# Half-width attention matmuls in alternation on the halves of TensorE's array, and k scores always in 32 bits

## The chip, the cores and the metric

One core of a Trainium2 chip runs the whole kernel. The metric is the device time of one execution in microseconds. Three runs of the kernel before took 1616.36, 1618.4 and 1621.14 us; the median, 1618.4, is the time before.

## What is computed

Three parts in a row, in float32 throughout:

```python
def sm_attn(qq, kk, vv):                       # softmax attention, 8 batches, 8 heads, head size 64
    s = scale * np.matmul(qq, kk.transpose(0, 1, 3, 2))
    s = s - np.max(s, axis=-1, keepdims=True)
    a = np.exp(s)
    a = a / (np.sum(a, axis=-1, keepdims=True) + 1e-09)
    return np.matmul(a, vv)
p_packed = sm_attn(p, k, v)                    # 32 packed queries against 576 keys
out = sm_attn(q, p_packed, p_packed)           # 576 queries against the 32 packed values
...
xk = mu_k * x + (1.0 - mu_k) * x_prev          # first MoE block, x_prev is x moved by one position
xr = mu_r * x + (1.0 - mu_r) * x_prev
k = np.maximum(xk @ w_k, 0.0)
x = 1.0 / (1.0 + np.exp(-(xr @ w_r))) * (k * k @ w_v)
...
h = x.transpose(0, 2, 1) @ U @ V               # second block, rank 32 over the positions
u = x + h.transpose(0, 2, 1)
u + np.maximum(u @ w_ch1, 0.0) @ w_ch2         # 512 to 2048 and back
```

## The kernel before, in words

**Units of attention.** The work of attention is cut into 16 units. Unit u holds two batches (a pair, `bp = u // 4`) and two heads (`j = u % 4`); in code the batch of the pair is `b2`. The two heads of 32 packed queries of one batch fill 64 partitions, and the two batches 128. `attention_steps` (line 641) writes one unit as a row of steps: turn k and p with TensorE transposes into `kh` and `pT`; scores of p against k into two banks of 288 columns (line 684); the exponentials into `a1`, which TensorE turns into `at`; `at` times v (line 739), scaled and masked to `pp`, which is copied to `ppz` (line 747) and turned to `ppt`; scores of q against `ppt` (line 762) and their softmax in `a2`, turned into `th`; and `ppz` times `th` into the output `xo` (line 803).

**Where the two batches of a pair stand on the array.** TensorE has 128 rows (the contraction) and 128 columns (the partitions of the result). For the scores of k, `pT` has four blocks of 64 columns, of which the two outer ones hold a batch each and the two inner ones zeros, so that each batch's 128-column weights fill its own 64 result partitions and add nothing to the others; the matmuls of both batches add up in one bank. `ppz` is laid out alike: `ppz[:, lh, b2, :]` has all 128 rows, those of the other batch being zero. Only `at` times v is written with 64-column weights into its half of the result partitions, first all four of batch 0 and then all four of batch 1.

**Plain and split units.** A matmul on 32-bit operands (F32) leaves two records for one instruction in the profile. The first seven units (`NPLAIN = 7`, "plain") use it everywhere. From unit 7 on ("split") the helper `halves` (line 653) writes an operand as two F32R tiles, its rounded value (on ACT) and the rest (on DVE): `kh` and `kl`, the two planes of `pT`, `th` and `tl`, the two planes of `ppz`. A product is then three one-record matmuls: high with high, high with low, low with high. The profile names all operands f32.

**Order of the work.** Everything is recorded in a `Plan` first, and `emit` (line 333) fixes each engine's program with a model of costs: an operation becomes ready when its inputs are, and of the ready ones the lowest class goes first, then the earliest recorded. Attention has class 0, the MoE blocks class 1, so a unit's matmuls are put among MoE matmuls, ahead of them when both are ready. `copy` (line 275) may go to ACT or DVE, whichever the plan has free. The first four units run interleaved at the start, with all eight PSUM banks (`att_banks`, line 542); after that attention has two banks, `ps_a`, given out in the order of the steps, and units 4 to 15 run under the chunks of the first MoE block, four for each pair of batches. The weights are cast and split on the way (`Cast`, line 821). Big tiles (`kin`, `qin`, `vin`, `kh`, `kl`, `qt`, `at`, `th`, `tl`, `xo`) rotate through one pool of eight buffers; all DMAs are issued on SP, and the loads for the next unit are recorded after the steps that free their tiles.

**Names in the profile.** Matmuls are recorded in one helper (line 197) and transposes in another (line 208), so groups are told apart by tiles: `psat` is attention's bank, `psk`, `psv`, `psr`, `psu` those of the first MoE block, `psc`, `psh`, `pst` those of the second.

Of the kernel before, what the change touches and what calls it, by code (L numbers as in the profile page):

```python
# [9 lines left out]
F32 = mybir.dt.float32  # L10
F32R = mybir.dt.float32r
# [458 lines left out]
def packed_attention_moe_mixer_kernel(  # L470
# [20 lines left out]
    P = 128  # L491
# [16 lines left out]
    plan = Plan(nc)  # L508
    add, sub, mul = ALU.add, ALU.subtract, ALU.mult
# [34 lines left out]
    def ps_att():  # L544
        return plan.bank(att_banks[0], "psat", att_banks[0] is ps_a)
# [17 lines left out]
    class Bufs:  # L563
# [13 lines left out]
            self.kept = None  # L577

        def keep(self, plain):

            if self.kept is None or self.kept[0] != plain:
                dt, n = (F32, 1 if self.first else 2) if plain else (F32R, 2)
                pT = plan.tile(self.one, [P, n, 4, 64], dt, "pT")
                ppz = plan.tile(self.one, [P, n, 2, P], dt, "ppz")
                for b2 in range(2):
                    r = slice(b2 * 64, (b2 + 1) * 64)
                    z = self.a1[r, 576 - b2 * 64:640 - b2 * 64].unsqueeze(1)
                    m = (1 if plain else 2) * 4
                    for t, v in ((pT, "p a b c -> p (a b) c"), (ppz, "p a b (e c) -> p (a b e) c")):
                        w = t[r, 0:m // 4].rearrange(v, **({} if t is pT else {"c": 64}))  # L590
                        plan.copy(w, z.to_broadcast([64, m, 64]), ("dve",))
                self.kept = (plain, pT, ppz)
            return self.kept[1:]

# [46 lines left out]
    def attention_steps(A, u, u_next):  # L641
# [3 lines left out]
            load_p(bp + 1)  # L645
        plan.tt(A.pbd, p_t[bp][:, j, :].unsqueeze(1).to_broadcast([P, 2, D]), hmask, mul)
        plain = u < NPLAIN
        kh = A.big(F32 if plain else F32R, "kh")
        kl = None if plain else A.big(F32R, "kl")
        qt, at = A.big(F32, "qt"), A.big(F32, "at")  # L650
        pT, ppz = A.keep(plain)

        def halves(hi, lo, src):
            if plain:
                plan.copy(hi, src)
            else:
                plan.act(hi, src, AF.Copy)
                plan.tt(lo, src, hi, sub)
# [3 lines left out]
        for b2 in range(2):  # L662
            yield
            ps = ps_att()
            for t in range(4):
                plan.transpose(ps[:, t * P:(t + 1) * P],
                               kin.at(b2)[:, b2 * 512 + t * P:b2 * 512 + (t + 1) * P], ident)
            sl = slice(b2 * 576, b2 * 576 + 512)
            halves(kh[:, sl], None if plain else kl[:, sl], ps)
        yield  # L670
        ps = ps_att()
        plan.transpose(ps[:, 0:P], kin[:, 1024:1152], ident)
        plan.transpose(ps[:, P:2 * P], A.pbd.rearrange("p h d -> p (h d)"), ident)
        pk_ = ps[:, 0:P].rearrange("p (b c) -> p b c", b=2)
        pp_ = ps[:, P:2 * P].rearrange("p (b c) -> p b c", b=2)
        khr = kh.rearrange("p (b c) -> p b c", b=2)[:, :, 512:576]
        halves(khr, None if plain else kl.rearrange("p (b c) -> p b c", b=2)[:, :, 512:576], pk_)
        halves(pT[:, 0, 0::3, :], None if plain else pT[:, 1, 0::3, :], pp_)
        if u_next is not None:
            A.load_k(u_next, A.after)  # L680

# [2 lines left out]
        for c in range(2):  # L684
            yield
            ps = ps_att()
            terms = []
            for b2 in range(2):
                ph = pT[:, 0, 2 * b2:2 * b2 + 2, :].rearrange("p a c -> p (a c)")
                pl = None if plain else pT[:, 1, 2 * b2:2 * b2 + 2, :].rearrange("p a c -> p (a c)")  # L690
                sl = slice(b2 * 576 + c * 288, b2 * 576 + (c + 1) * 288)
                terms += [(ph, kh[:, sl])] if plain else [(ph, kh[:, sl]), (ph, kl[:, sl]), (pl, kh[:, sl])]
            for n, (lh, rh) in enumerate(terms):
                plan.mm(ps[:, 0:288], lh, rh, start=(n == 0), stop=(n + 1 == len(terms)))
            plan.reduce(st[:, c:c + 1], ps[:, 0:288], ALU.max)
            sps.append(ps)
        plan.tt(st[:, 2:3], st[:, 0:1], st[:, 1:2], ALU.max)
# [5 lines left out]
        for b2 in range(2):  # L703
            r = slice(b2 * 64, (b2 + 1) * 64)
# [6 lines left out]
        for c in range(3):  # L711
            yield
            ps = ps_att()
            for t in range(3):
                i = 3 * c + t
                plan.transpose(ps[:, t * P:(t + 1) * P], qin[:, i * P:(i + 1) * P], ident)
            n = 3 if c < 2 else 2
# [9 lines left out]
        ps = ps_att()  # L727
# [4 lines left out]
        ps = ps_att()  # L732
# [3 lines left out]
        yield  # L736
        ps = ps_att()
        vm = vin[:, 0:1024].rearrange("p (b h t d) -> p b h t d", b=2, h=2, t=4)
        for b2 in range(2):
            for t in range(4):  # L740
                plan.mm(ps[b2 * 64:(b2 + 1) * 64, 0:P],
                        at[:, t * P + b2 * 64:t * P + (b2 + 1) * 64], vm[:, b2, :, t, :],
                        start=(t == 0), stop=False, skip_group_check=True)
        plan.mm(ps[:, 0:P], at[:, 512:640], vin[:, 1024:1152], start=False, stop=True, skip_group_check=True)
        pp = plan.tile(A.one, [P, P], F32, "pp")
        plan.stt(pp, ps[:, 0:P], st[:, 9:10], hmask.rearrange("p h d -> p (h d)"), mul, mul)
        for b2 in range(2):
            r = slice(b2 * 64, (b2 + 1) * 64)
            plan.copy(ppz[r, 0, b2, :], pp[r])
            if not plain:  # L750
                plan.tt(ppz[r, 1, b2, :], pp[r], ppz[r, 0, b2, :], sub)
        if u_next is not None:
            A.load_v(u_next, A.after)
        yield
        ps = ps_att()
# [33 lines left out]
        th = A.big(F32 if plain else F32R, "th")  # L789
        tl = None if plain else A.big(F32R, "tl")  # L790
        yield
        ps = ps_att()
# [4 lines left out]
        ps = ps_att()  # L797
        plan.transpose(ps[:, 0:P], a2g[:, 512:640], ident)
        for b2 in range(2):
            r = slice(b2 * 64, (b2 + 1) * 64)  # L800
            halves(th[r, 512:576], None if plain else tl[r, 512:576], ps[r, r])
        xo = A.big(F32, "xo", (0, 1)).rearrange("p (i b c) -> p i b c", i=NI, b=2)
        for b2 in range(2):
            for c0, c1 in ((256, 576), (0, 256)):
                yield
                ps = ps_att()
                w = c1 - c0
                terms = ((0, th),) if plain else ((0, th), (0, tl), (1, th))
                for n, (lh, rh) in enumerate(terms):
                    plan.mm(ps[:, 0:w], ppz[:, lh, b2, :], rh[:, c0:c1], start=(n == 0),  # L810
                            stop=(n + 1 == len(terms)))
                plan.copy(xo.on(b2)[:, c0 // 64:c1 // 64, b2, :],
                          ps[:, 0:w].rearrange("p (i c) -> p i c", c=64))
        plan.dma(x_d[bp].at(j)[j * P:(j + 1) * P, :], xo.rearrange("p i b c -> p (i b c)"))

    def attention(A, u, u_next):
        for _ in attention_steps(A, u, u_next):
            pass
# [93 lines left out]
    plan.cls = 0  # L912
    A0.after = go
    steps = [attention_steps(AX_[u], u, NJ if u == 0 else None) for u in range(NJ)]
    step = 0
    while any(s is not None for s in steps):
# [38 lines left out]
    for b2 in range(2):  # L955
        r = slice(b2 * 64, (b2 + 1) * 64)
        z = A0.a1[r, 576 - b2 * 64:608 - b2 * 64]
# [263 lines left out]
    for n in range(len(chunks)):  # L1221
        b, c = chunks[n]
# [48 lines left out]
    for n in range(len(chunks)):  # L1271
        prep = []
        if n + 1 < len(chunks):
            b1, c1 = chunks[n + 1]
# [4 lines left out]
        for m in range(MC + 2):  # L1279
# [6 lines left out]
            if m >= 6 and prep:  # L1286
                kind, a = prep.pop(0)
# [42 lines left out]
```

## Time and profile before

| what | value |
|---|---|
| median of three runs | 1618.4 us (1616.36 to 1621.14) |
| the profiled execution | 1620.91 us |
| its span, first to last instruction | 1619.1 us |
| busy: PE, DVE, ACT, POOL | 1559.5, 800.2, 616.8, 3.0 us |
| granted TensorE clock, mean over the span | 0.985 of 2.4 GHz |
| DMA | 128.57 MB, 79 GB/s over the span |

PE is TensorE's matmuls, PEld its weight loads. A PE record lasts from its start to its modelled end, latency included, and the next starts before it ends; the time that a matmul takes from the engine is the distance between two starts. A row of the windows table has the stretch, its length in us, and then, for each engine that has work there, in the order PE, PEld, DVE, ACT, POOL, the busy us and in brackets the number of records in flight; the last three numbers are the granted clock (PEclk, 1.00 is 2.4 GHz), the busy share of the 16 DMA engines and GB/s. A row of the timeline has the start in us, the time from the first start to the last end of the records merged in it, the engine, and what they are; "128*64" is the part of the array that is used, rows by columns, and "128x288" the operand that moves through it, partitions by elements. `psat<-kh,pT` reads: written `psat`, read `kh` and `pT`.

### The profile page before, as it was taken

The numbers are of one execution on the slowest core, as the hardware profiler recorded it, in microseconds if no ns is written. First come the engines' busy times: TensorE is split into PE (matmuls) and PEld (weight loads), VectorE is DVE, ScalarE is ACT, GpSimd is POOL, SyncE is SP. The second block draws the span as 40 slices with busy tenths as digits, with TensorE's granted clock in tenths as the row PEclk, the third lists the DMA queues.
The fourth block names the chain that finished last, engine by engine and source line by source line (L and its number), as shares of the span: only waits on it lengthen the run. The fifth ranks groups of instructions, "written<-read, shape, count | busy, mean of one in ns | idle before, by whom it ended". The sixth has DMA issues, their size and how long they took to land.

```text
span 1619.1 us, 21662 instructions
## 1 busy us (share of the span) xinstructions
PE 1559.5 (96%) x8152; PEld 1384.9 (86%) x8152; DVE 800.2 (49%) x2035; ACT 616.8 (38%) x1442; POOL 3.0 (0%) x18
## 2 busy tenths in 40 slices
PE   7777889999999999999999999999999999999998
PEld 6566778888888888888889999999999989999997
DVE  5879887887888778764532222222222222221211
ACT  4767666666766666554321111111111111111110
POOL 0000000000000000000000000000000000000000
PEclk9889899999999999999999999999999999999999
DMA  9965445456453333330511101010010101101000
GB/s 184 214 165 140 124 123 137 136 137 168 132 134 122 128 93 112 109 108 20 167 61 46 46 1 39 1 46 13 27 39 1 40 1 40 40 0 40 0 20 20
DMA packets 156393, 128.57 MB, mean 79 GB/s; under 512 B 94145, under 2 KB 121473, under 8 KB 156289
## 3 DMA queue, kind: packets, MB, share of 16 engines
q1 hardware_dynamic: 156288, 127.19, 27.9%
q8 instruction: 64, 1.05, 0.3%
q14 instruction: 41, 0.33, 0.1%
HBM read 89.33 MB, written 37.82 MB: 79 GB/s over the span
## 4 chain that ended last, share of the span: by engine, by line
PE 91%; DVE 3%; ACT 2%; DMA 2%; SPq 1%; issue 1%; ACTq 0%; DVEq 0%
PE psc L197 49%; PE psv L197 12%; PE psk L197 12%; PE psr L197 6%; PE psat L197 6%; PE psat L208 2%; SPq L311 1%; PE psu L197 1%; PE psh L197 1%; PE pst L208 1%; ACT a L229 1%; DMA qin<-in_q_dram 1%; DMA s<-w_d 0%; DVE h L265 0%; DVE m L250 0%
## 5 line engine op out<-in xcount | busy, mean ns | idle before, releaser
L197 PE MATMUL psc<-ut,w 128*128 128x384 f32 x2304 | 433.9, 338 | 1.0 <-DVE hid L265 1.0
L197 PE MATMUL psc<-w,hid 128*128 128x512 f32 x1728 | 426.1, 393 | 1.1 <-ACT hid L229 1.1
L197 PEld LDWEIGHTS psc<-ut,w 128*128 128x128 f32 x2304 | 405.5, 188 | 13.1 <-DVE hid L265 1.4
L197 PEld LDWEIGHTS psc<-w,hid 128*128 128x128 f32 x1728 | 322.0, 188 | 60.9 <-ACT hid L229 1.5
L265 DVE SCALAR_TENSOR_TENSOR hid<-psc,hid 128x384 fp32r<-128x384 f32 x192 | 106.9, 557 | 466.1 <-ACT hid L229 466.0
L229 ACT ACTIVATE hid<-psc 128x384 fp32r<-128x384 f32 x192 | 94.2, 491 | 607.5 <-PE psc L197 607.5
L197 PE MATMUL psv<-wv,kk 128*128 128x512 f32 x864 | 227.9, 400 | 3.7 <-DVE wv L250 3.7
L197 PE MATMUL psk<-xk,wk 128*128 128x384 f32 x1152 | 227.7, 341 | 1.0 <-DVE xk L250 1.0
L197 PEld LDWEIGHTS psk<-xk,wk 128*128 128x128 f32 x1152 | 202.1, 189 | 7.6 <-DVE xk L250 1.5
L197 PEld LDWEIGHTS psv<-wv,kk 128*128 128x128 f32 x864 | 159.4, 189 | 32.9 <-DVE wv L250 4.3
L197 PE MATMUL psr<-wr,xr 128*128 128x512 f32 x432 | 111.0, 403 | 4.6 <-ACT xr L280 4.6
L197 PEld LDWEIGHTS psr<-wr,xr 128*128 128x128 f32 x432 | 81.6, 193 | 21.3 <-ACT xr L280 4.9
L250 DVE TENSOR_TENSOR kk<-sq,kk 128x384 fp32r<-128x384 f32 x96 | 52.6, 553 | 46.1 <-ACT kk L280 45.5
L229 ACT ACTIVATE sq<-psk 128x384 f32<-128x384 f32 x96 | 46.4, 486 | 69.4 <-PE psk L197 67.7
L229 ACT ACTIVATE m<-x,om_t 128x384 f32<-128x384 f32 x96 | 57.2, 610 | 12.3 <-DVE xk L250 6.0
L262 DVE SCALAR_TENSOR_TENSOR m<-x,mu_t,m 128x384 f32<-128x384 f32 x96 | 57.9, 611 | 3.8 <-ACT m L229 3.6
L250 DVE TENSOR_TENSOR ut<-pst,ut 128x512 fp32r<-128x512 f32 x36 | 24.9, 691 | 67.4 <-ACT ut L229 67.3
L229 ACT ACTIVATE a<-st 128x256 f32<-128x256 f32 (+2 forms) x109 | 45.8, 427 | 23.2 <-DVE m L250 16.5
L250 DVE TENSOR_TENSOR u<-psh,u 128x512 f32<-128x512 f32 x36 | 24.9, 691 | 51.0 <-PE psh L197 47.8
L229 ACT ACTIVATE m<-st 128x256 f32<-128x256 uint32 (+2 forms) x109 | 45.2, 426 | 7.1 <-DVE wv L250 2.7
L250 DVE TENSOR_TENSOR o<-psc,u 128x512 f32<-128x512 f32 x36 | 24.6, 688 | 46.5 <-PE psc L197 44.7
L229 ACT ACTIVATE ut<-pst 128x512 fp32r<-128x512 f32 x36 | 21.5, 598 | 67.6 <-PE pst L208 67.6
(134 smaller groups left out, 1527.3 us busy)
## 6 DMA issues: line engine op xcount, KB each, us to landing
st<-in_moe_w_ch_dram SPq DMA_DIRECT2D x64, 256.0 KB, 2.8
qin<-in_q_dram SPq DMA_DIRECT2D x32, 288.0 KB, 5.3
x_d<-xo SPq DMA_DIRECT2D x16, 576.0 KB, 3.4
x_d<-x SPq DMA_DIRECT2D x36, 256.0 KB, 3.7
u<-x_d SPq DMA_DIRECT2D x36, 256.0 KB, 3.4
out_dram<-o SPq DMA_DIRECT2D x36, 256.0 KB, 2.0
kin<-in_k_dram SPq DMA_DIRECT2D x32, 256.0 KB, 4.5
vin<-in_v_dram SPq DMA_DIRECT2D x32, 256.0 KB, 4.7
```

Source lines behind the costliest of these rows:

```text
L197: self.nc.tensor.matmul(o, l, r, start=start, stop=stop, **k)
L208: self.nc.tensor.transpose(out.get(), in_.get(), ident.get())
L229: self.nc.scalar.activation(o, in_.get(), func, **k)
L250: return self.elem(engs, lambda e, o, x, y: e.tensor_tensor(out=o, in0=x, in1=y, op=op), out, [a, b], self.TT, cls)
L262: ("dve",), lambda e, o, x, y, z: e.scalar_tensor_tensor(out=o, in0=x, scalar=z, in1=y, op0=op0, op1=op1), out, [a, b, s], {"dve": (1.042, ...
L265: ("dve",), lambda e, o, x, y: e.scalar_tensor_tensor(out=o, in0=x, scalar=s, in1=y, op0=op0, op1=op1), out, [a, b], self.TT, cls)
L311: self.nc.sync.dma_start(out=o, in_=i)
```

## The change

- `pT` holds one 32-bit block of 64 columns for each batch, with no zero blocks, and the scores of k become two matmuls for each 288 columns, one into each half of the result partitions (64 columns of the array). This holds for split units too, so `kl` and the low plane of `pT` are gone.
- `at` times v runs over the four pieces outside and the batches inside, so the halves alternate.
- `ppz` holds `pp` once, with no zeros, and is copied once instead of once per batch. The last product takes the 64 rows of each batch from `ppz` and `th`, one batch into each of two banks, alternating; both banks are asked for before the first matmul, and both are copied out after the last.
- The zero fills of `pT` and `ppz` are gone.

```diff
--- before.py
+++ after.py
@@ -577,18 +577,10 @@
             self.kept = None
 
         def keep(self, plain):
-
             if self.kept is None or self.kept[0] != plain:
                 dt, n = (F32, 1 if self.first else 2) if plain else (F32R, 2)
-                pT = plan.tile(self.one, [P, n, 4, 64], dt, "pT")
-                ppz = plan.tile(self.one, [P, n, 2, P], dt, "ppz")
-                for b2 in range(2):
-                    r = slice(b2 * 64, (b2 + 1) * 64)
-                    z = self.a1[r, 576 - b2 * 64:640 - b2 * 64].unsqueeze(1)
-                    m = (1 if plain else 2) * 4
-                    for t, v in ((pT, "p a b c -> p (a b) c"), (ppz, "p a b (e c) -> p (a b e) c")):
-                        w = t[r, 0:m // 4].rearrange(v, **({} if t is pT else {"c": 64}))
-                        plan.copy(w, z.to_broadcast([64, m, 64]), ("dve",))
+                pT = plan.tile(self.one, [P, 2, 64], F32, "pT")
+                ppz = plan.tile(self.one, [P, n, P], dt, "ppz")
                 self.kept = (plain, pT, ppz)
             return self.kept[1:]
 
@@ -645,8 +637,7 @@
             load_p(bp + 1)
         plan.tt(A.pbd, p_t[bp][:, j, :].unsqueeze(1).to_broadcast([P, 2, D]), hmask, mul)
         plain = u < NPLAIN
-        kh = A.big(F32 if plain else F32R, "kh")
-        kl = None if plain else A.big(F32R, "kl")
+        kh = A.big(F32, "kh")
         qt, at = A.big(F32, "qt"), A.big(F32, "at")
         pT, ppz = A.keep(plain)
 
@@ -666,7 +657,7 @@
                 plan.transpose(ps[:, t * P:(t + 1) * P],
                                kin.at(b2)[:, b2 * 512 + t * P:b2 * 512 + (t + 1) * P], ident)
             sl = slice(b2 * 576, b2 * 576 + 512)
-            halves(kh[:, sl], None if plain else kl[:, sl], ps)
+            plan.copy(kh[:, sl], ps)
         yield
         ps = ps_att()
         plan.transpose(ps[:, 0:P], kin[:, 1024:1152], ident)
@@ -674,8 +665,8 @@
         pk_ = ps[:, 0:P].rearrange("p (b c) -> p b c", b=2)
         pp_ = ps[:, P:2 * P].rearrange("p (b c) -> p b c", b=2)
         khr = kh.rearrange("p (b c) -> p b c", b=2)[:, :, 512:576]
-        halves(khr, None if plain else kl.rearrange("p (b c) -> p b c", b=2)[:, :, 512:576], pk_)
-        halves(pT[:, 0, 0::3, :], None if plain else pT[:, 1, 0::3, :], pp_)
+        plan.copy(khr, pk_)
+        plan.copy(pT, pp_)
         if u_next is not None:
             A.load_k(u_next, A.after)
 
@@ -684,14 +675,10 @@
         for c in range(2):
             yield
             ps = ps_att()
-            terms = []
             for b2 in range(2):
-                ph = pT[:, 0, 2 * b2:2 * b2 + 2, :].rearrange("p a c -> p (a c)")
-                pl = None if plain else pT[:, 1, 2 * b2:2 * b2 + 2, :].rearrange("p a c -> p (a c)")
-                sl = slice(b2 * 576 + c * 288, b2 * 576 + (c + 1) * 288)
-                terms += [(ph, kh[:, sl])] if plain else [(ph, kh[:, sl]), (ph, kl[:, sl]), (pl, kh[:, sl])]
-            for n, (lh, rh) in enumerate(terms):
-                plan.mm(ps[:, 0:288], lh, rh, start=(n == 0), stop=(n + 1 == len(terms)))
+                plan.mm(ps[b2 * 64:(b2 + 1) * 64, 0:288], pT[:, b2, :],
+                        kh[:, b2 * 576 + c * 288:b2 * 576 + (c + 1) * 288],
+                        start=True, stop=True, skip_group_check=True)
             plan.reduce(st[:, c:c + 1], ps[:, 0:288], ALU.max)
             sps.append(ps)
         plan.tt(st[:, 2:3], st[:, 0:1], st[:, 1:2], ALU.max)
@@ -736,19 +723,17 @@
         yield
         ps = ps_att()
         vm = vin[:, 0:1024].rearrange("p (b h t d) -> p b h t d", b=2, h=2, t=4)
-        for b2 in range(2):
-            for t in range(4):
+        for t in range(4):
+            for b2 in range(2):
                 plan.mm(ps[b2 * 64:(b2 + 1) * 64, 0:P],
                         at[:, t * P + b2 * 64:t * P + (b2 + 1) * 64], vm[:, b2, :, t, :],
                         start=(t == 0), stop=False, skip_group_check=True)
         plan.mm(ps[:, 0:P], at[:, 512:640], vin[:, 1024:1152], start=False, stop=True, skip_group_check=True)
         pp = plan.tile(A.one, [P, P], F32, "pp")
         plan.stt(pp, ps[:, 0:P], st[:, 9:10], hmask.rearrange("p h d -> p (h d)"), mul, mul)
-        for b2 in range(2):
-            r = slice(b2 * 64, (b2 + 1) * 64)
-            plan.copy(ppz[r, 0, b2, :], pp[r])
-            if not plain:
-                plan.tt(ppz[r, 1, b2, :], pp[r], ppz[r, 0, b2, :], sub)
+        plan.copy(ppz[:, 0, :], pp)
+        if not plain:
+            plan.tt(ppz[:, 1, :], pp, ppz[:, 0, :], sub)
         if u_next is not None:
             A.load_v(u_next, A.after)
         yield
@@ -800,17 +785,19 @@
             r = slice(b2 * 64, (b2 + 1) * 64)
             halves(th[r, 512:576], None if plain else tl[r, 512:576], ps[r, r])
         xo = A.big(F32, "xo", (0, 1)).rearrange("p (i b c) -> p i b c", i=NI, b=2)
-        for b2 in range(2):
-            for c0, c1 in ((256, 576), (0, 256)):
-                yield
-                ps = ps_att()
-                w = c1 - c0
-                terms = ((0, th),) if plain else ((0, th), (0, tl), (1, th))
-                for n, (lh, rh) in enumerate(terms):
-                    plan.mm(ps[:, 0:w], ppz[:, lh, b2, :], rh[:, c0:c1], start=(n == 0),
+        for c0, c1 in ((256, 576), (0, 256)):
+            yield
+            w = c1 - c0
+            pss = [ps_att() for _ in range(2)]
+            terms = ((0, th),) if plain else ((0, th), (0, tl), (1, th))
+            for n, (lh, rh) in enumerate(terms):
+                for b2 in range(2):
+                    r = slice(b2 * 64, (b2 + 1) * 64)
+                    plan.mm(pss[b2][:, 0:w], ppz[r, lh, :], rh[r, c0:c1], start=(n == 0),
                             stop=(n + 1 == len(terms)))
+            for b2 in range(2):
                 plan.copy(xo.on(b2)[:, c0 // 64:c1 // 64, b2, :],
-                          ps[:, 0:w].rearrange("p (i c) -> p i c", c=64))
+                          pss[b2][:, 0:w].rearrange("p (i c) -> p i c", c=64))
         plan.dma(x_d[bp].at(j)[j * P:(j + 1) * P, :], xo.rearrange("p i b c -> p (i b c)"))
 
     def attention(A, u, u_next):
```

## Rows read from the trace of the kernel before

**Rows 1.** Windows table, four stretches: length, busy us (records) per engine, PEclk, DMA share, GB/s.

```profile
0.00:60.00 60.00, 46.56 (x284) 38.21 (x285) 39.74 (x144) 32.37 (x101) 1.32 (x11) 0.94 0.96 197
60.00:240.00 180.00, 144.80 (x759) 118.09 (x758) 155.52 (x492) 122.75 (x332) 0.00 (x0) 0.90 0.55 145
240.00:540.00 300.00, 296.79 (x1707) 262.96 (x1707) 242.97 (x676) 199.44 (x484) 0.22 (x2) 1.00 0.49 135
540.00:1619.00 1079.00, 1071.36 (x5408) 965.68 (x5406) 361.93 (x724) 262.27 (x528) 1.45 (x5) 1.00 0.14 46
```

**Rows 2.** Waits of PE, 240 to 1619: us in total, times, longest.

```profile
PE psu L197 <- DVE xs L283: 2.6, 6, 0.5
```

**Rows 3.** Chain of waits, 60 to 240, shares by line.

```profile
by line: PE psat L197 17.5%; PE psk L197 9.1%; PE psv L197 9.0%; PE psr L197 8.4%; PE psat L208 5.5%; ACT a L229 5.4%; issue 3.6%; DMA qin<-in_q_dram 3.5%; DVE h L265 2.5%; DVE m L250 2.5%; DMA st<-in_moe_w_k_dram 2.3%; DVE a L265 2.1%; ACT
```

**Rows 4.** Windows table of tile kl alone.

```profile
60.00:240.00 180.00, 2.36 (x8) 1.51 (x8) 3.32 (x6) 0.90 0.55 145
240.00:540.00 300.00, 8.27 (x28) 5.25 (x28) 11.59 (x21) 1.00 0.49 135
```

**Rows 5.** Windows table of tile vin alone.

```profile
60.00:240.00 180.00, 11.06 (x90) 9.25 (x90) 0.90 0.55 145
```

**Rows 6.** Timeline of PE, unit 10: start, us to the last end, work.

```profile
298.32 2.00 PE L197 MATMUL psat<-vin,at 128*64 128x128 f32 x18
300.07 0.48 PE L197 MATMUL psv<-wv,kk 128*128 128x512 f32 x1
```

**Rows 7.** Tile vin: shortest, median, longest record in ns.

```profile
L197 PE MATMUL psat<-vin,at x288: 272/273/476, 21.2 to 497.8; 128*64 128x128 f32 x128, 128*128 128x128 f32 x16
```

**Rows 8.** Windows table of tile vin, within the block of rows 6 (counts all in flight).

```profile
298.80:299.20 0.40, 0.40 (x10) 0.40 (x9) 1.00 0.00 0
299.20:299.64 0.44, 0.44 (x9) 0.44 (x5) 1.00 0.49 130
```

**Rows 9.** Timeline of PE, scores of unit 11 (split).

```profile
324.20 0.30 PE L197 MATMUL psat<-kh,pT 128*128 128x288 f32 x1
...
324.86 0.30 PE L197 MATMUL psat<-kl,pT 128*128 128x288 f32 x1
...
326.32 0.51 PE L197 MATMUL psk<-xk,wk 128*128 128x384 f32 x2
```

**Rows 10.** Timeline of PE, scores of a plain unit.

```profile
110.54 2.11 PE L197 MATMUL psat<-kh,pT 128*128 128x288 f32 x8
```

**Rows 11.** Timeline of PE, whole array to halves and back.

```profile
55.61 0.64 PE L208 MATMUL psat<-ident,a 128*128 128x128 f32 x4
56.18 1.09 PE L197 MATMUL psat<-vin,at 128*64 128x128 f32 x8
57.19 0.33 PE L208 MATMUL psat<-ident,a 128*128 128x128 f32 x1
```

**Rows 12.** Timeline of PE, packed values to output of unit 10 (split).

```profile
314.90 0.31 PE L197 MATMUL psat<-th,ppz 128*128 128x320 f32 x1
...
315.40 0.31 PE L197 MATMUL psat<-tl,ppz 128*128 128x320 f32 x1
...
316.04 1.09 PE L197 MATMUL psv<-wv,kk 128*128 128x512 f32 x4
316.97 0.31 PE L197 MATMUL psat<-th,ppz 128*128 128x320 f32 x1
...
317.77 0.40 PE L197 MATMUL psv<-wv,kk 128*128 128x512 f32 x1
```

**Rows 13.** Timeline of PE, second scores (128-column weights, 64 columns moving).

```profile
302.13 2.17 PE L197 MATMUL psat<-ppt,qt 128*128 128x64 f32 x18
```

**Rows 14.** Timeline of PE, packed values to output of a plain unit.

```profile
58.91 2.11 PE L197 MATMUL psat<-th,ppz 128*128 128x320 f32 x8
```

**Rows 15.** Tile ppz: shortest, median, longest in ns.

```profile
L280 ACT ACTIVATE ppz<-pp x28: 292/307/313, 36.0 to 500.2; 64x128 fp32r<-64x128 f32 x16, 64x128 f32<-64x128 f32 x12
```

**Rows 16.** Tile xo: shortest, median, longest in ns.

```profile
L280 ACT ACTIVATE xo<-psat x53: 376/393/456, 48.0 to 516.2; 128x256 f32<-128x256 f32 x27, 128x320 f32<-128x320 f32 x26
```

## The prediction

> **What bounds the kernel now.** First the windows table over four stretches [rows 1]: from 240 us to the end PE is busy 99% at the full granted clock (1.00, which is 2.4 GHz), while DVE falls from 81% (240 to 540) to 34% (after 540). Then who PE waits for after 240: the largest entry is 2.6 us [rows 2]. So from 240 us on TensorE is the bound, and a microsecond of it that is saved is a microsecond of the end. Between 60 and 240 us no engine is full: PE 80%, DVE 86%, granted clock 0.90 [rows 1]; since the clock has two levels, 1.2 and 2.4 GHz, 0.90 means a fifth of that stretch at the lower one. Its chain of waits gives attention's matmuls and transposes 23% and spreads the rest over the MoE blocks, DVE, ACT and DMA [rows 3]. Up to 60 us the DMA engines are 96% busy [rows 1]. After 540 there is no attention.
>
> Where the units lie: kl is written three times by each unit of the split kind; it has 21 records in 240 to 540 and 6 in 60 to 240 [rows 4], so seven and two such units. The at-by-v product has 18 records in a unit, and 90 in 60 to 240 [rows 5], so that stretch holds five units, three of them plain. The other four of the 16 lie under the loads of the first 60 us.
>
> **The change part by part**, in time between starts on PE (a record's shown duration includes its latency, so the cost is the start-to-start distance).
>
> (a) *at by v, alternated.* Now the block starts at 298.32 and the next work starts at 300.07, 1.75 us for 18 records [rows 6]. A 32-bit matmul leaves two records, and these start 0.11 us apart: 18 records in a line take 17 distances and the 0.27 that one is in flight [rows 7], 2.14, where the row shows 2.00. The trace says why: in a line, with 0.27 us in flight each, a window of 0.40 us would hold six; the window from 298.80 holds 10, and the next, 0.44 us long, 9 [rows 8]. The halves of the array thus do already work side by side, for about three distances of the block: the second half starts before the first has all its records. Alternated, two streams of eight run beside each other: 8 x 0.109 + 0.10 for the first weight load and the offset = 0.97. Now it is 1.75 less 0.33, for two full-width records of 0.11 and the exit before them (about 0.1, see b) = 1.42. **0.45 us saved per unit.**
>
> The Trainium skill (TensorE: Matmul & The Clock Gate, Part 3, "What overlaps and what doesn't") says that matmuls start and end strictly in program order. The trace does not agree: 10 records in 0.40 us can't be one line [rows 8]. By that rule the sum below would be 3.4 us smaller; what it would do here is worked out as a rival.
>
> (b) *The score product, two 64-column halves in 32 bits.* Split units now: eleven records from 324.86 to 326.32, 0.133 apart, and one at 324.20: 1.46 + 0.13 = 1.59 us [rows 9]. After: four matmuls, eight records. A 288-column 32-bit record has a distance of (2.11 - 0.40) / 7 = 0.244 [rows 10]. Side by side that is four slots, 0.98, and 0.06 offset. New is the switch between whole array and halves: an `a` transpose's last start is 55.61 + 0.64 - 0.27 = 55.98 and the half-width work starts at 56.18, 0.20 later where 0.11 is usual; the last of these eight starts at 57.00 and the next whole-array record at 57.19 [rows 11]. So 0.09 each way, 0.18 for a visit. Sum 1.22, **0.37 saved**. Ends: all in a line 8 x 0.244 + 0.18 = 2.13, a loss of 0.54; no offset at all, 0.43 saved. I take nearly the upper end, since (a)'s windows show 32-bit column halves side by side. A plain unit goes from 8 x 0.244 = 1.95 to 1.22, 0.73 saved.
>
> (c) *Packed values to output, two 64-row halves.* Split units now: 0.15 + (316.04 - 315.40) + (317.77 - 316.97) = 1.59 us, 12 records [rows 12]; the stretch from 316.97 to 317.77 holds three of each width, so six slots are 0.80 us. After: six pairs in six slots, 0.80, in three visits: the first term is ready before its low half (MoE matmuls stand between 314.90 and 315.40), and the second column range must wait until both banks are empty, since the pair takes both of attention's two banks at once. Each visit costs 0.18 of switches and an estimated 0.10 for a weight load that can't be fetched ahead over the switch (about one distance of a load, below): 0.80 + 3 x 0.28 = 1.64. No row has row halves, so ends: two visits with nothing but switches, 0.80 + 0.36 = 1.16, a gain of 0.43; weight loads that don't run side by side, which the 64-column scores bound (18 records in 2.17 us, 0.11 each although half as long as at-by-v's, so the load of 128 columns sets it [rows 13]): 12 x 0.11 + 0.84 = 2.16, a loss of 0.57. I take the middle, **0.05 lost**. A plain unit now takes 2 x 0.97 = 1.94 (eight records in 2.11 with latency [rows 14]); 0.97 + 0.56 = 1.53 after, 0.41 saved.
>
> (d) *DVE and ACT.* kl goes (3.3 us of DVE in 60 to 240, 11.6 in 240 to 540 [rows 4]), the low half of pT, the zero fills of pT and ppz, and one of two ppz copies of 0.31 [rows 15]; kh may now go to either engine. From 240 on this is worth nothing: PE's largest wait there is 2.6 us [rows 2]. The exposed step is the second pair of banks: both evacuations, 0.39 each [rows 16], stand before the next matmul where they used to lie beside it. MoE matmuls fill PE meanwhile; without them (60 to 240) it costs up to 0.5 a unit, 2.5 us. No DMA is added and none is moved past another on SP; the tile rotation loses one tile a unit, so loads come no later.
>
> **The sum.** 240 to 540: 7 x (0.45 + 0.37 - 0.05) = 5.4 us. 60 to 240: PE loses 3 x (0.45 + 0.73 + 0.41) + 2 x 0.77 = 6.3 us of work, and DVE and ACT lose some 5 (kl 3.3, five ppz copies 1.6); what of it counts lies between a loss of 3 (banks, with nothing gained) and 6.3. I take 3: attention has a quarter of the chain there, the engines that lose work hold most of the rest, and none is full. 0 to 60: nothing, the DMA covers it; if that cover is thin, 1 us. Together **8.4 us**. The profiled execution took 1620.9 us (span 1619.1 and 1.8 around it), so 1612.5 beside it; it lies 2.5 above the median of the three runs, 1618.4, and against that the forecast is **1610.0**.
>
> **Rivals.**
> - *Row halves load their weights in a line.* (c) costs 0.57 a unit: 7 x 0.25 = 1.8 from 240 on, and about 1 before: 1615.6, no change that can be told. For it: in [rows 13] loads bound the short records. Against: the two halves load from different partitions. Chance 0.24.
> - *Going from one row half to the other drains the array*, as going from whole to halves does. Then the twelve records stand in a line, 1.59, with some ten changes of 0.09 between the halves and three visits of 0.28: 1.59 + 0.9 + 0.84 = 3.3, a loss of 1.7 in each split unit against 0.82 gained in (a) and (b), and about 1.5 against 1.2 in a plain one. 12 units lose: 7 x 0.9 + 2 x 0.9 + 3 x 0.3 = 9, less the 3 or so from shorter DVE work: 1624, slower. It decides from the point where (c) takes over 2.4 us. Against: [rows 8] show column halves without it. Chance 0.08.
> - *Records start strictly in order.* A 32-bit matmul is two records; the second waits for the first of its own half and holds up the other half behind it, so an alternated block needs one slot more: (a) loses 0.11 and (b) 0.24, 0.35 x 7 = 2.4 from 240 on and 1 before: 1613.4. Against: [rows 8]. Chance 0.08. The Trainium skill's rule named under (a) would have it so.
> - *The middle stretch is shorter by all its PE work lost*, since DVE and ACT hand weights and mixes on earlier: 6.3 instead of 3, and a microsecond at the start: 1605.7. For it: DVE is the busiest there. Against: part of the chain is DMA, and the granted clock, already 0.90 there [rows 1] with PE idle a fifth of the time; if less matmul work took it to 0.88, 0.02 x 180 = 3.6 us would be given back. Chance 0.13.
> - *The halves don't pair at all in (b) and (c)*, only (a) gains: 7 x (0.45 - 0.54 - 0.6) is a loss of 5, less 3 gained before 240: 1620, no change. Chance 0.05.
>
> **How the numbers follow.** My forecast has the remaining 0.42, with an own range of 1606 to 1614 (the half of (c)'s ends, and 2 us of the middle stretch). About 0.3%, 5 us, is what a measurement of this kernel can tell from no change: faster means under 1613.5. That takes nine tenths of the forecast (0.38), the last-but-one rival (0.13), half of the in-order rival (0.04) and a sixth of the first (0.04): 0.59. Slower (over 1623.3) is the drain rival and a sliver, 0.08. Same, 0.33. The range of eight in ten runs from 1604 to 1618.
>
> **What would show it.** (a) right: at-by-v from its first record to the next work in 1.3 us instead of 1.75. (b) right: eight records within 1.3 us. (c): the time of its visits against 1.6 a unit; 2.2 would be loads in a line, over 3 a drain. Stretch: the MoE blocks end of attention's units some 5 us earlier relative to 240. The prediction is wrong if half-width records stand 0.24 apart, if PE's waits after 240 grow over 5 us, or if the granted clock before 240 moves by more than 0.03.

## The result and the profile after

The changed kernel takes 1604.84 us (median of four runs, 1601.54 to 1607.12) beside 1619.15 us for the kernel before on the same chip: a ratio of 0.9911, interval 0.9886 to 0.9937. That is 14.3 us less; the forecast was 8.4 less. The result lies at the fast edge of the forecast's wide range (1604 to 1618), and outside its own narrower one (1606 to 1614).

Where the time went shows first in the table of four stretches (columns as in [rows 1]), the changed kernel:

```profile
0.00:60.00 60.00, 44.84 (x286) 33.79 (x287) 36.41 (x128) 32.45 (x100) 1.33 (x11) 0.91 0.96 194
60.00:240.00 180.00, 148.08 (x840) 114.04 (x840) 161.09 (x521) 131.33 (x353) 0.00 (x0) 0.90 0.61 159
240.00:540.00 300.00, 298.96 (x1673) 252.21 (x1672) 238.58 (x666) 200.68 (x479) 0.23 (x2) 1.00 0.50 141
```

From 60 to 240 us more is done: 840 matmul records against 759, and DVE, which lost work, is busier than before (161.1 us against 155.5), with 521 instructions done against 492: more of its other work has come through. The second MoE block then starts earlier by 16.8 us and takes as long as before, as the tile `psc` shows (shortest, median and longest record in ns, then the first and last start):

```profile
L197 PE MATMUL psc<-ut,w x2304: 333/334/442, 761.3 to 1589.6; 128*128 128x384 f32 x192
```

In the kernel before this row reads 778.1 to 1606.9. So 16.8 of the 17.6 us between the spans of these two executions are won before 778 us.

The three blocks that the change rewrites, each in a late unit, one of the seven that run after 240 us. First at by v (timeline, columns as in [rows 6]):

```profile
343.88 1.51 PE L197 MATMUL psat<-vin,at 128*64 128x128 f32 x18
345.14 0.42 PE L197 MATMUL psk<-xk,wk 128*128 128x384 f32 x1
```

1.26 us from its start to the next work, against 1.75 [rows 6]. The windows of the same block show both halves at work throughout, 8 and 14 records in flight in 0.40 us where one line has six [rows 8]:

```profile
343.90:344.30 0.40, 0.40 (x8) 0.40 (x10) 1.00 0.91 287
344.30:344.70 0.40, 0.40 (x14) 0.40 (x8) 1.00 1.10 374
```

The scores of k:

```profile
333.52 1.19 PE L197 MATMUL psat<-kh,pT 128*64 128x288 f32 x8
334.64 0.74 PE L197 MATMUL psv<-wv,kk 128*128 128x512 f32 x2
```

Eight records in 1.12 us. The second row holds a cost that the prediction left out: of two psv records in 0.74 us, with about 0.40 in flight each, the second starts 0.34 after the first, where the usual distance is 0.23. The first work behind a switch pays 0.11 for a weight load that wasn't fetched ahead.

The last product of the same unit:

```profile
325.18 0.41 PE L197 MATMUL psat<-th,ppz 64*128 64x320 f32 x1
325.52 0.50 PE L197 MATMUL psv<-wv,kk 128*128 128x512 f32 x1
325.95 0.41 PE L197 MATMUL psat<-th,ppz 64*128 64x320 f32 x1
325.95 0.56 PE L197 MATMUL psat<-tl,ppz 64*128 64x320 f32 x2
326.21 0.45 PE L197 MATMUL psat<-th,ppz 64*128 64x320 f32 x2
326.58 1.19 PE L197 MATMUL psr<-wr,xr 128*128 128x512 f32 x4
327.71 0.38 PE L197 MATMUL psat<-th,ppz 64*128 64x256 f32 x1
327.93 0.28 PE L197 MATMUL psat<-tl,ppz 64*128 64x256 f32 x1
328.05 0.28 PE L197 MATMUL psat<-th,ppz 64*128 64x256 f32 x1
328.26 0.49 PE L197 MATMUL psr<-wr,xr 128*128 128x512 f32 x1
328.68 0.39 PE L197 MATMUL psat<-th,ppz 64*128 64x256 f32 x1
328.91 0.28 PE L197 MATMUL psat<-tl,ppz 64*128 64x256 f32 x1
329.03 0.27 PE L197 MATMUL psat<-th,ppz 64*128 64x256 f32 x1
329.23 0.50 PE L197 MATMUL psr<-wr,xr 128*128 128x512 f32 x1
```

Four visits. In the first a single record stands alone; in the last two the two halves don't run beside each other at all: three records of one batch, a whole-array matmul, three of the other. (A visit is one stretch of half-width work between whole-array work.) The plan asks for two banks, but a matmul only waits for its own, so the first half goes as soon as its bank is there. With 0.09 for the way in and 0.11 behind the way out the visits cost 0.34 + 0.20, 0.63 + 0.20, 0.55 + 0.20 and 0.55 + 0.20, together 2.87 us, against 1.59 [rows 12]. Of the seven late units three have four visits and four have three (2.1 us).

PE's waits from 240 on (the row of [rows 2], after):

```profile
PE psu L197 <- DVE xs L283: 1.0, 2, 0.5
```

### The profile page after: what moved, and what is told of

It reads as the page before. It is cut to its first block, busy times and chain, and to the rows that moved or that the text cites. A ratio compares the mean times of both kernels' runs of the same rounds, so it can differ in the third digit from the quotient of the medians.

```text
span 1601.5 us, 21551 instructions
## 1 busy us (share of the span) xinstructions
PE 1546.4 (97%) x8116; PEld 1350.1 (84%) x8116; DVE 775.7 (48%) x1966; ACT 615.7 (38%) x1428; POOL 3.0 (0%) x18
## 4 chain that ended last, share of the span: by engine, by line
PE 92%; DVE 2%; DMA 2%; ACT 2%; SPq 2%; issue 1%; ACTq 0%; DVEq 0%
PE psc L197 49%; PE psk L197 13%; PE psv L197 12%; PE psr L197 6%; PE psat L197 5%; PE psat L208 3%; SPq L311 2%; PE psu L197 1%; PE psh L197 1%; PE pst L208 1%; DMA qin<-in_q_dram 1%; ACT a L229 1%; DVE s L269 0%; DMA s<-w_d 0%; DVE m L250 0%
## 5 line engine op out<-in xcount | busy, mean ns | idle before, releaser
L265 DVE SCALAR_TENSOR_TENSOR h<-a,st 128x256 f32<-128x256 f32 (+2 forms) x109 | 44.7, 414 | 5.9 <-ACT a L229 5.3
```

The lines of the kernel that those rows point to most:

```text
L265: ("dve",), lambda e, o, x, y: e.scalar_tensor_tensor(out=o, in0=x, scalar=s, in1=y, op0=op0, op1=op1), out, [a, b], self.TT, cls)
```

## The experiments

**How far each kernel is at 240 us.** To split a kernel's gain I count the work that TensorE has started by 240 us: each record at the start-to-start distance that it has in the trace of the kernel before (psk 0.174 us, psv 0.231, psr 0.227, psu 0.232, a transpose 0.109, second scores 0.111; per unit 1.42 for the half-width records of at by v, 1.59 or 1.95 for the first scores, 1.59 or 1.94 for the last product), whatever it costs in the kernel at hand. The kernel before has started 154.2 us of such work. The lead of a kernel is the difference to that; its final lead is read from the first start of `psc` against 778.1. Each lead comes from one profiled execution, and executions of the same kernel differ by some us, so a lead is good to a few us and no more.

The expectations weigh three theories of the middle stretch, 60 to 240 us. *Matmul time*: each us of matmul work that is removed counts in full. *Relief*: what counts is the work taken from DVE and ACT. *Order*: the new costs made the plan put the work in another order, and the gain is that order's.

**One part at a time.** First the loops of at by v alone:

```diff
-        for b2 in range(2):
-            for t in range(4):
+        for t in range(4):
+            for b2 in range(2):
                 plan.mm(ps[b2 * 64:(b2 + 1) * 64, 0:P],
```

> The kernel before with only the loops of at by v swapped, so that the halves alternate. In the trace of the changed kernel this block takes 1.27 us instead of 1.75. If matmul time removed counts in full in every unit after the start (theory of matmul time): 12 units x 0.49 = 5.9 us less, about 1613. If work before 240 us only counts through DVE and ACT (theory of relief): 7 x 0.49 = 3.4 us less, about 1615.5. If the middle stretch of the changed kernel owes its gain to the order that the plan came to (theory of order): the stretch up to 240 us may move by some 5 us either way, whatever was removed.

Measured: ratio 0.9975 (0.9964 to 0.9986). The lead at 240 us is -0.2 us, and the final one 3.2. So in this order the matmul time that the units lost before 240 bought nothing there, and seven late units bought 3.4, which is 7 x 0.49. The middle stretch keeps its picture too (row 60 to 240, as in [rows 1]):

```profile
60.00:240.00 180.00, 142.30 (x759) 115.26 (x758) 156.63 (x499) 123.17 (x332) 0.00 (x0) 0.90 0.58 148
```

759 matmul records, as many as before; PE is just busy 2.5 us less.

Then the scores alone:

```diff
-        kh = A.big(F32 if plain else F32R, "kh")
-        kl = None if plain else A.big(F32R, "kl")
+        kh = A.big(F32, "kh")
...
-                plan.mm(ps[:, 0:288], lh, rh, start=(n == 0), stop=(n + 1 == len(terms)))
+                plan.mm(ps[b2 * 64:(b2 + 1) * 64, 0:288], pT[:, b2, :],
+                        kh[:, b2 * 576 + c * 288:b2 * 576 + (c + 1) * 288],
+                        start=True, stop=True, skip_group_check=True)
```

> The kernel before with only the scores of k on column halves in 32 bits, and so without kl, the low plane of pT and the zero fill of pT. Matmul time: split units 0.38 x 9, plain units after the start 0.74 x 3, 5.6 us less, about 1613.5. Relief: this is the part that takes the most from DVE (kl and pT, about 1.9 us a split unit, and a fill), so 2.7 us from the seven late units and 8 or more up to 240, about 1608.

Measured: 0.9923 (0.9903 to 0.9944), a lead of 7.2 us at 240. By itself nearly as much as the whole change, and nearer to the value of the theory of relief. Here DVE's relief and the shorter score matmuls come together, so this kernel doesn't separate the two.

The last product alone:

```diff
-                ppz = plan.tile(self.one, [P, n, 2, P], dt, "ppz")
+                ppz = plan.tile(self.one, [P, n, P], dt, "ppz")
...
-                    plan.mm(ps[:, 0:w], ppz[:, lh, b2, :], rh[:, c0:c1], start=(n == 0),
+                    plan.mm(pss[b2][:, 0:w], ppz[r, lh, :], rh[r, c0:c1], start=(n == 0),
```

> The kernel before with only the last product on row halves, ppz copied once and not filled with zeros. In the trace of the changed kernel a late split unit pays 1.8 us for it where both halves of the second range stand together and 2.5 where they don't, against 1.59 before. Matmul time: 7 x 0.5 lost after 240, about 1 gained before it from the plain units, about 1621. Relief: one copy and one subtraction fewer a unit is 0.6 us a unit on ACT and DVE, about 1618 to 1620.

Measured: 0.9991 (0.998 to 1.0002), a lead of -2.3 us at 240 and of -2.1 at the end. It buys nothing that can be told from zero. Nor does the loss of 7 x 0.5 us after 240 show that matmul time expected: from there on the lead grew by 0.2. PE sat idle for 1.6 us instead of 3.2 from 240 to 540, which makes up for part of the loss; the rest is open.

**DVE's work put back.** The changed kernel, in which DVE and ACT do what they did before, into tiles that nobody reads:

```diff
-            plan.copy(kh[:, sl], ps)
+            halves(kh[:, sl], None if plain else kl[:, sl], ps)
...
-        plan.copy(ppz[:, 0, :], pp)
-        if not plain:
-            plan.tt(ppz[:, 1, :], pp, ppz[:, 0, :], sub)
+        for b2 in range(2):
+            r = slice(b2 * 64, (b2 + 1) * 64)
+            plan.copy(ppz[r, 0, :], pp[r])
+            if not plain:
+                plan.tt(ppz[r, 1, :], pp[r], ppz[r, 0, :], sub)
```

> The changed kernel with the work of DVE and ACT that the change removed put back, its results unused: the zero fills, kl and the low part of pT in split units, and ppz written in two halves. TensorE's work is that of the changed kernel. Matmul time: as the changed kernel, 1604 to 1607. Relief: the middle stretch loses its gain again, 1611 to 1614. Order: anything between, with the middle stretch some us off either way.

Measured: 0.995 (0.9933 to 0.9967), a lead of 3.7 us at 240 instead of 13.1. The total, 8 us less than before, lies between what relief and matmul time expect, nearer to relief. Its middle stretch:

```profile
60.00:240.00 180.00, 144.87 (x771) 108.62 (x768) 162.11 (x512) 125.62 (x340) 0.00 (x0) 0.85 0.57 148
```

DVE is as full as in the changed kernel, 162 us, but TensorE has only 771 records instead of 840. That alone doesn't show relief: the granted clock is 0.85 here and 0.90 in the changed kernel, and 0.05 of 180 us is 9 us at the full clock, as much as the 9.4 us of lead that this kernel lacks. It also puts `kl` back among the eight rotating tiles, so that the loads may wait for a tile again; that was not tried by itself.

**What the order alone is worth.** The plan's model of costs decides the order. These kernels change only that model, by a few ns, once for the kernel before and once for the changed one:

```diff
-            return f * max(f * n / 2.4, 107.0) + 3.0
+            return f * max(f * n / 2.4, 107.0) + 5.0
```

> The kernel before; only the plan's cost of a matmul is 5 ns above the streaming time instead of 3, so that the same work is put in a slightly different order. It measures what the order alone is worth. Theories of relief and of matmul time: within 3 us of before. Theory of order: 5 us or more off, up to 240 us.

> The changed kernel with the same 2 ns in the plan's matmul cost. Relief and matmul time: within 3 us of the changed kernel, about 0.991 of before. Theory of order: some of the 13 us that the changed kernel is ahead at 240 us is gone, 0.994 or more.

Measured: 0.9964 (0.9951 to 0.9977) for the kernel before and 0.9957 (0.9942 to 0.9972) for the changed one. With this order the change is worth nothing. The expectation of both theories was missed. That of the order was met in the totals; for the kernel before, 3.0 of its 5.8 us lie before 240. The lead of the changed kernel at 240 us falls from 13.1 to 1.7, with PE as busy but at a lower granted clock, 0.82:

```profile
60.00:240.00 180.00, 147.95 (x759) 113.44 (x759) 153.31 (x488) 119.98 (x325) 0.00 (x0) 0.82 0.57 151
```

So I took two further orders of each: a second with the same constant at 1, a third with another price for a transpose.

```diff
-            return f * max(f * n / 2.4, 107.0) + 3.0
+            return f * max(f * n / 2.4, 107.0) + 1.0
```

```diff
-            return 110.0
+            return 114.0
```

> The kernel before, the plan's matmul cost 1 ns above the streaming time instead of 3: a second other order of the same work. With the two plans run so far the kernel before stands at 1 and 0.996. Relief: 0.995 to 1.003, and at 240 us within 4 us of the kernel before in work done.

> The changed kernel in the same second order. Its two plans so far stand at 0.991 and 0.996. If the relief of DVE is real, the mean over four plans of the changed kernel is ahead of that of the kernel before by some 10 us, of which 4 are matmul time after 240; this one then comes out at 0.989 to 0.994. If the gain of the middle stretch was the order's, the two means differ by 4 us and this one comes out at 0.994 to 1.

> The kernel before, the plan's cost of a transpose 114 ns instead of 110: a third other order. As for the second: 0.995 to 1.003.

> The changed kernel in the third order. As for the second: 0.989 to 0.994 if the relief is real, 0.994 to 1 if the middle stretch's gain was the order's.

Measured: 0.997 (0.996 to 0.9979) and 0.9928 (0.9911 to 0.9944) in the second order, 0.9959 (0.9944 to 0.9973) and 0.9947 (0.993 to 0.9963) in the third. Both of the kernel before are as expected; of the changed kernel, the second order fell where relief was to put it, the third where the order was. Of its four orders the kernel before was first timed in the slowest, the changed kernel in the fastest. The means are 0.9973 and 0.9936, each with a standard deviation of 0.002, so the difference is 0.0037 with an interval of 0.0004 to 0.0071 (four values a side, t for 6 degrees of freedom). That is 6 us (0.6 to 11.5) for the change and some 8 for the order in the pair that was first timed. Relief was to give about 10 us between the means, the order 4; the interval holds both, so four orders a side don't decide between them.

**Other last products.** The changed kernel with the last product, and the layout of ppz, as before:

```diff
-                    plan.mm(pss[b2][:, 0:w], ppz[r, lh, :], rh[r, c0:c1], start=(n == 0),
+                    plan.mm(ps[:, 0:w], ppz[:, lh, b2, :], rh[:, c0:c1], start=(n == 0),
```

> The changed kernel with the last product as before: zero-filled ppz, all 128 rows, two copies of ppz a unit. Matmul time: the late units get back 0.5 us each, 3.5 us faster than the changed kernel after 240. Relief: the fill (0.8 us) and a copy and a subtraction a unit come back in the middle stretch, some 2 to 3 us of DVE and ACT work, so about as fast as the changed kernel, 0.989 to 0.992 of before.

Measured: 0.9897 (0.9881 to 0.9914); lead 5.1 us at 240 and 13.5 at the end. From 240 on it wins 8.4 us where the changed kernel wins 3.7. The ratio is within relief's range; the 4.7 us it gains on the changed kernel after 240 are near the 3.5 of matmul time.

And the row halves kept together:

```diff
-            terms = ((0, th),) if plain else ((0, th), (0, tl), (1, th))
+            terms = ((0, th),) if plain else ((0, tl), (0, th), (1, th))
...
-                            stop=(n + 1 == len(terms)))
+                            stop=(n + 1 == len(terms)), after=[x.alloc for x in pss])
```

> The changed kernel with the row halves kept together: the first matmul waits for both banks, and the product that needs the low half of th comes first, so that no term is ready before the others. Two visits a unit, six records in alternation in each. By the changed kernel's visits (0.64 and 0.55 us, and 0.09 for the way in) 1.4 us a unit instead of about 2.1: 7 x 0.7 = 4.8 us less after 240. Matmul time and relief agree here; before 240 theory of relief expects nothing, matmul time 1 us more. 0.987 to 0.989 of before.

Measured: 0.9905 (0.9886 to 0.9924), so the expected 0.987 to 0.989 was missed. The intervals of these two and of the changed kernel overlap, so none of the three is shown to be the best. The timeline of the paired kernel shows two visits, each with all six records in pairs:

```profile
365.06 0.34 PE L197 MATMUL psk<-xk,wk 128*128 128x384 f32 x1
365.33 0.42 PE L197 MATMUL psat<-tl,ppz 64*128 64x320 f32 x2
365.58 0.47 PE L197 MATMUL psat<-th,ppz 64*128 64x320 f32 x4
365.98 1.49 PE L197 MATMUL psk<-xk,wk 128*128 128x384 f32 x7
367.40 0.39 PE L197 MATMUL psat<-tl,ppz 64*128 64x256 f32 x2
367.62 0.40 PE L197 MATMUL psat<-th,ppz 64*128 64x256 f32 x4
367.95 0.44 PE L197 MATMUL psk<-xk,wk 128*128 128x384 f32 x1
```

0.65 and 0.55 us, and 0.20 for each visit's ways in and out: 1.60. That is no less than the 1.59 of twelve whole-array records [rows 12], where the expectation had 1.4. In a split unit row halves save six slots of 0.13 and pay for four switches and the loads behind them.

**All kernels beside each other.** Ratio, lead at 240 us, and granted clock from 60 to 240:

| kernel | ratio | lead at 240 | clock |
|---|---|---|---|
| before | 1 | 0 | 0.90 |
| before, other orders (three) | 0.9964, 0.997, 0.9959 | 3.0, -2.5, 1.7 | 0.91, 0.86, 0.92 |
| at by v alone | 0.9975 | -0.2 | 0.90 |
| last product alone | 0.9991 | -2.3 | 0.87 |
| changed, DVE's work back | 0.995 | 3.7 | 0.85 |
| scores alone | 0.9923 | 7.2 | 0.90 |
| changed | 0.9911 | 13.1 | 0.90 |
| changed, other orders (three) | 0.9957, 0.9928, 0.9947 | 1.7, 8.6, 4.8 | 0.82, 0.86, 0.87 |
| changed, old last product | 0.9897 | 5.1 | 0.90 |
| changed, rows paired | 0.9905 | 9.5 | 0.88 |

The seven kernels in which kl's work stays on DVE have a mean lead of 0.5 us (standard deviation 2.4); the seven without it 7.1 (3.7). At by v alone, which shortens matmuls in the same stretch, lies with the first seven. This speaks for a gain from DVE's relief, but it does not show it. The same grouping separates the kernels with the old scores from those with the new ones, except for the kernel with DVE's work back, which stands in one order; and its 3.7 lies inside the spread of the changed kernel's four orders.

The clock column holds a rival. Among the orders of one kernel the lead goes with the granted clock: 1.7 at 0.82, 8.6 and 4.8 at 0.86 and 0.87, 13.1 at 0.90 for the changed kernel; -2.5 at 0.86 and 0 to 3.0 at 0.90 to 0.92 for the kernel before. One and the same kernel shows it as well: two executions of the kernel before in its third order took 1609.99 us at a mean clock of 0.995 and 1618.86 at 0.987. Much of what an order is worth thus comes with the clock, and the kernel with DVE's work back, 3.7 at 0.85, lies where the changed kernel's orders would put it at that clock. Whether the clock makes the lead, or a TensorE that waits more loses the clock, no run here shows.

## Why the prediction was right or wrong

**The total** was right for the change, but not for the reason written. 8.4 us were forecast, 14.3 measured in the first pair, about 6 as the mean over four orders of each. The range has no term for the order; nothing in it says that 2 ns in the plan's model move this kernel by 6 us. It is the largest thing that was missed, and the reason why the first pair alone would have been read as proof of a larger effect. That the forecast came near is partly luck: its 5.4 us after 240 were not what the matmuls gave there, and its 3 us before 240 were more than doubled.

**(a) at by v**: 0.45 forecast, 0.49 measured, in every late unit; seven of them gave 3.4 us by themselves. The reading of [rows 8], that the halves already overlapped for part of the block, was right.

**(b) the scores**: 0.37 forecast. The block itself is as forecast, 1.12 and the way in; but the 0.11 behind the way out was left out, so 1.32 a visit and 0.27 saved. The two halves do run side by side in 32 bits.

**(c) the last product** is the step that failed, as a term of the sum: a loss of 0.05 a late unit was forecast, and the loss was 0.5 with three visits and 1.3 with four, 6 us over seven units. Neither rival on the row halves was the cause. In the paired kernel's timeline two records start within 0.01 us of each other, so there is no drain between halves; and weight loads of 128 columns do run side by side: the sixth record starts at 365.58 + 0.47 less the 0.31 that one is in flight, 365.74, which is 0.41 after the first, where five loads of 0.11 ahead of the sixth would take 0.55. By the prediction's own sign the 2.1 us of a unit with three visits would read as loads in a line; the timeline shows that it is not that.

What cost was the price of a visit, and records without a partner. The prediction priced a visit at 0.28 on top of its slots. It costs about 0.40: the switches, 0.09 each way; 0.11 for the load behind the way out, which the prediction left out; and 0.10 inside, since the second pair stands 0.25 behind the first (365.33 to 365.58) where a slot is 0.15, its loads not fetched ahead either. The paired kernel agrees: 1.60 less 0.80 for six slots is two visits of 0.40. In the changed kernel the first visit holds a single record, which takes a slot of its own: 0.80 + 0.15 + 3 x 0.40 = 2.15, where about 2.13 was measured. In three units the plan also pulled the halves of the second column range apart: a fourth visit, and three slots more of 0.12, together 2.9, where 2.87 was measured.

So from 240 us on the matmuls gave 7 x (0.49 + 0.27) - 6, about nothing, instead of 5.4. The changed kernel's lead still grew by 3.7 us there; PE's idle time between 240 and 540 fell by 2.2 us, from 3.2 [rows 1] to 1.0, which is a part of it. The prediction put DVE's relief at nothing here because these waits are small; whether relief or the order shortened them isn't shown. The three other orders of the changed kernel grew by 2.1 to 2.2, those of the kernel before by 0.2 to 4.5. Without the row halves the same stretch gave 8.4.

**The middle stretch**: 3 us forecast from a range of -3 to 6.3, 13.1 measured in the first pair and 6.5 as the difference of means over four orders (7.05 against 0.55). The interval of that difference, -0.2 to 13.2 (four values a side, as above), just reaches zero. The step that is in doubt is pricing the stretch by the matmul work, of which part was to count: at by v alone shows that in its order none of its matmul work counted there. DVE and ACT lost 5 us of work by the prediction's own count, 3.3 of it `kl` on DVE, the busiest engine, and that is near the mean that came. But this is argued, not shown, as long as the clock and the order aren't separated from it. The rival of a shorter middle stretch had its argument, that DVE is the busiest there, in the text with a chance of 0.13.

**Its counterweight**, the granted clock, also stood there, and it shows: the seven kernels with row halves have a mean clock of 0.864 between 60 and 240 us, the seven without 0.899. Over 180 us the difference is 6.3 us at the full clock. The two groups overlap: the changed kernel has 0.90 with row halves, the kernel before 0.86 without them in one order. What in the last product the clock follows, if it does, was not tried.

**Records strictly in order**, the third rival, did not come, as the chance of 0.08 had it. At by v is issued as two records of batch 0, two of batch 1, and so on; with 14 records in flight in 0.40 us and pairs 6 ns apart, the first record of batch 1 starts with the first of batch 0, ahead of the second.

## What to carry to other kernels

Where a plan of many thousand instructions is made by a model of costs, change that model by a nanosecond or two and time the same work in some other orders, before and after, ahead of crediting a change of under one per cent; here the order was worth as much as the change. Set the granted clock of the stretch beside each time, since here the lead went with it. Half-width matmuls pay where many records stand together in alternation; each change between the whole array and its halves cost 0.09 us and 0.11 more for the load behind it, so a visit with three short pairs wins nothing. In the stretch where DVE was the busiest, shorter matmuls of at by v bought nothing in the one order that was tried; price what a change takes from the busiest engine there as well, though these runs don't show that this is what paid.

## What was not expected of the hardware

Two halves of the array start a pair 5 to 7 ns apart for column halves in 32 bits, and within 8 ns for row halves in the changed kernel. The Trainium skill (TensorE: Matmul & The Clock Gate, Part 3, "Measured speedup vs the span model") gives about 4 ns per tile, and the trace is near it. Its page TensorEngine Tiling (Array Packing), "Key Properties", says that changing the tiling mode drains the engine while changing the tile doesn't; the traces agree, with 0.09 us at each change, and add that the next weight load can't be fetched over it, 0.11 us more, which falls on the work of somebody else and so hides from a reading of the changed block alone.
